# Moving a state transpose, splitting a weight cast and reordering two groups of matmuls in an attention-and-MLP kernel

## The chip, the cores and the metric

The kernel runs on one core of a Trainium2 chip. The metric is the device time in microseconds. Five engines work side by side, each through its own queue in order: TensorE (PE in the profile, with its weight loads as PEld), VectorE (DVE), ScalarE (ACT), GpSimd (POOL) and SyncE (SP, which here only issues DMAs). An instruction that waits holds up all that stands behind it on its engine.

## The reference

`x` has 8 batches of 8 heads with 512 rows of 64, `state` 8 x 8 x 32 x 64. Each attends to the other, and the joined result goes through an MLP:

```python
scores = scale * np.matmul(x, state.transpose(0, 1, 3, 2))
a = softmax(scores)                      # over the 32 states
xread = np.matmul(a, state)
scores2 = scale * np.matmul(state, x.transpose(0, 1, 3, 2))
a2 = softmax(scores2)                    # over the 512 rows of x
sread = np.matmul(a2, x)
y = np.concatenate([xread, sread], axis=2)   # to (8 * 544) tokens x 512
h = y @ w_in                             # 512 x 2048
out = (h * sigmoid(h)) @ w_out           # 2048 x 512
```

(`softmax` stands for the lines that subtract the maximum, take the exponential and divide by the sum.)

## The kernel before, in words

The 512 token columns are cut into 4 pairs of heads (`kt`), the 2048 hidden columns into 16 tiles (`ft`), the 512 x-rows of a batch into 4 output tiles (`tt`). The kernel does not form xread: it folds state into w_in. For each batch it forms `W1 = state @ w_in` (`w1_m` L274, evicted by `w1_e` L299, four quarters `j` of 512 columns), and then `g1` (L309) multiplies the attention weights `aT` with `W1` and ACT applies silu, 128 hidden columns at a time; `g2` (L335) multiplies with `w_out` and sums over `ft` in PSUM. The sread rows are collected in `xsT` and go through the MLP at the end as a ninth batch.

The whole order is written by hand inside `tc.manual_schedule()` (L368): the order of the Python calls is the order of each engine's queue. Waits between engines come from the tiles that instructions share. PSUM has eight banks, `o0 o1 w0 w1 h0 h1 a0 a1`, and calls name the bank they use.

What bears on the change:

- **Loads.** SP issues x of batch 0 in four parts, state 1 into `st_f[1]` (L373), the first quarter of `w_in` in four rows into `w_f` (L375), then a quarter of `w_out` (L430). POOL's queue issues the other weights and x of batches 1 and 2 (L94, L100, L105), between its own casts. From batch 3 on SP issues x (`load_x`, L92), one 1 MB DMA per batch, at L567 and L626, behind the DMA transposes of x (`x_Td`) and among the output stores (`o_e` L354).
- **First softmax (L418 to L463).** Casts of x, PE transposes (`x_T` L139, evicted by `x_Te`), scores (`sc` L171), exponentials (`ex` L183, ACT), row sums and normalisation (DVE and POOL).
- **First W1 (L470 to L478).** `w1f_m` multiplies rows 0 and 1 of `w_f` in fp32. Rows 2 and 3 are cast to bf16 in `w_in_sb` by ACT (L473) and DVE (L474), and `w1_m(0, 0, ..., (2, 3))` reads them. `a_T` (L222) transposes the weights of batch 0 with one eviction on DVE and one on ACT.
- **Start of the MLP (L487 to L500).** `g1(0, 0)`, `g1(0, 1)`, `sread_m` (L239), two more `g1`. On DVE stand the casts of rows 0 and 1 of `w_f` (L491), `sread_n` (L254, which writes `sr`), and the cast of state 1 into `st_nat` (L493). On PE stand `st_T(1)` (L120: a transpose of `st_nat` at L122, two copies into `sbd` by DVE), `G2(0, 0)`, which is `g2` for all four `tt`, and `sread_t` (L264), which transposes `sr`. POOL meanwhile casts four tiles of `w_out_sb` (L468).
- **Batch 1 (L513 to L547).** `cast_x`, `xTs` (L404: two `x_T` and one DVE eviction into `xT`), `scs` (L409), an EXP table load on ACT, `exs` (L400), a SILU table load, `norm_s` and `norm_m` (L193, L198), with `g1` and `G2` of batch 0 between them. `W1x(0, 3, HB, DD)` (L538) forms the last quarter of W1 of batch 0, evicted by two DVE casts.
- **Phases 1 to 8 (L646).** `g2` of one batch with the next batch's steps filled in at the step numbers of `plan` (L613). `soft(b)` casts x of batch b + 1 on POOL (`cast_xu`).

Of the kernel before, what the change touches and what calls it, by code (L numbers as in the profile page):

```python
# [19 lines left out]
def kernel(  # L20
# [8 lines left out]
    nc = tc.nc  # L29
# [13 lines left out]
    st_f = [pers.tile([128, 128], FP32, name=f"st_f{i}") for i in range(2)]  # L43
    w_f = pers.tile([128, KT, 512], FP32, name="w_f")
    wo_f = pers.tile([128, 4, DM], FP32, name="wo_f")
    sbd_f = pers.tile([128, KT, NS], FP32, name="sbd_f")
    st_nat = pers.tile([128, B, 128], BF16, name="st_nat")
# [15 lines left out]
    w_in_sb = pers.tile([128, KT, DF], BF16, name="w_in_sb")  # L63
# [13 lines left out]
    def bf(name):  # L77
        return bank[name][:].bitcast(BF16)

    def cp(eng, dst, src):  # L80
        if eng == "dve":
            nc.vector.tensor_copy(dst, src)  # L82
        elif eng == "pool":
            nc.gpsimd.tensor_copy(dst, src)  # L84
        else:
            nc.scalar.activation(dst, src, func=COPY, bias=0.0)  # L86


    def x_src(b, kt, n):
        return x[b, ds(2 * kt, 2 * n)].rearrange("h (p c) d -> p h (c d)", c=4)  # L90

    def load_x(b, eng, kt=0, n=4):  # L92
        dst = x_f[b % 2][:, ds(kt, n)].rearrange("p k h e -> p (k h) e")
        eng.dma_start(dst, x_src(b, kt, n))  # L94
# [25 lines left out]
    def st_T(b, bk, e0, e1):  # L120
        v = bf(bk)[:, 0:128]
        nc.tensor.transpose(v, st_nat[:, b, :], ident[:])  # L122
        for half, e in ((0, e0), (1, e1)):
            cp(
                e,
                sbd[ds(64 * half, 64), b, :, half, :],
                v[ds(64 * half, 64)].rearrange("p (ns kt) -> p kt ns", kt=KT),
            )
# [10 lines left out]
    def x_T(b, kt, bk):  # L139
        v = bf(bk).rearrange("p (k c t) -> p k c t", k=2, c=4)  # L140
        for c in range(4):
            nc.tensor.transpose(
                v[:, kt % 2, c, :], x_n[b % 2][:, kt, c, ds(2, 128)], ident[:]
            )

    def x_Te(b, kt, n, bk, eng):
        v = bf(bk).rearrange("p (k c t) -> p k c t", k=2, c=4)
        cp(eng, xT[b % 2][:, ds(kt, n)], v[:, ds(kt % 2, n)])
# [22 lines left out]
    def sc(b, kt, bk):  # L171
        v = bank[bk][:].rearrange("p (k h c s) -> p k h c s", k=2, h=2, c=4)
        for c in range(4):
            nc.tensor.matmul(  # L174
                v[:, kt % 2, :, c, :],
                xT[b % 2][:, kt, c, :],
                sbd[:, b, kt, :, :],
                start=True,
                stop=True,
                skip_group_check=True,  # L180
            )

    def ex(b, kt, n, bk):  # L183
        v = bank[bk][:].rearrange("p (k q s) -> p k q s", k=2, q=8)
        nc.scalar.activation(  # L185
            en[b % 2][:, :, :, ds(kt, n), :].rearrange("p h c k s -> p k (h c) s"),
            v[:, ds(kt % 2, n)],
            func=EXP,
            bias=0.0,
            scale=SCALE,  # L190
        )
# [6 lines left out]
    def norm_m(b, eng, kt=0, n=4, h0=0, hn=2):  # L198
        e = nc.vector if eng == "dve" else nc.gpsimd
        e.tensor_tensor(  # L200
            an[b % 2][:, ds(h0, hn), :, ds(kt, n), :].rearrange("p h c k s -> p (h c) k s"),
            en[b % 2][:, ds(h0, hn), :, ds(kt, n), :].rearrange("p h c k s -> p (h c) k s"),
            rs[b % 2][:, ds(h0, hn), :, ds(kt, n)]
            .rearrange("p h c k -> p (h c) k")
            .unsqueeze(3)
            .to_broadcast([128, 4 * hn, n, NS]),
            op=MULT,
        )
# [13 lines left out]
    def a_T(b, bks):  # L222
        n = 2 // len(bks)
        for i, (bk, e) in enumerate(bks):
            v = bf(bk).rearrange("p (h c t) -> p h c t", h=2, c=4)
            for half in range(n):
                for c in range(4):
                    nc.tensor.transpose(
                        v[:, half, c, :], an[b % 2][:, i * n + half, c, :, :], ident[:]
                    )  # L230
            cp(e, aT[b % 2][:, ds(i * n, n)], v[:, ds(0, n)])
# [55 lines left out]
    def w1f_m(bks, kt):  # L287
        for half in range(2):
            nc.tensor.matmul(
                bank[bks[half]][ds(32 * kt, 32), :],  # L290
                sbd_f[ds(64 * half, 64), kt, :],
                w_f[ds(64 * half, 64), kt, :],
                start=True,
                stop=True,
                skip_group_check=True,
                tile_position=(64 * half, 32 * kt),
            )
# [11 lines left out]
    def g1(b, ft):  # L309
        bk = bank[f"h{hctr[0] % 2}"]  # L310
        hctr[0] += 1
        if b < B:
            for half in range(2):
                nc.tensor.matmul(  # L314
                    bk[:],
                    W1[b % 2][:, half, ds(128 * ft, 128)],
                    aT[b % 2][:, half, :, :],
                    start=(half == 0),
                    stop=(half == 1),
                    skip_group_check=True,  # L320
                )
            nc.scalar.activation(g[b % 2][:, ft, :], bk[:], func=SILU, bias=0.0)  # L322
        else:
            for kt in range(KT):
                nc.tensor.matmul(  # L325
                    bk[:, 0:256],
                    w_in_sb[:, kt, ds(128 * ft, 128)],
                    xsT[:, kt, :, :, :],
                    start=(kt == 0),
                    stop=(kt == KT - 1),  # L330
                    skip_group_check=True,
                )
            nc.scalar.activation(g_s[:, ft, :], bk[:, 0:256], func=SILU, bias=0.0)  # L333

    def g2(b, tt, ft, bk, cols=(0, 512)):  # L335
        src = g[b % 2] if b < B else g_s
        c0, c1 = cols
        nc.tensor.matmul(  # L338
            bank[bk][:, c0:c1],
            src[:, ft, ds(128 * tt, 128)],  # L340
            w_out_sb[:, ft, c0:c1],
            start=(ft == 0),
            stop=(ft == 15),
            skip_group_check=True,
        )
# [15 lines left out]
    def warm(n, bk, w=128):  # L361
        for i in range(n):
            nc.tensor.matmul(
                bank[bk][:, 0:w], zeros[:, 0:128], zeros[:, 0:w], start=True, stop=True,
                skip_group_check=True,
            )

    with tc.manual_schedule():  # L368
# [23 lines left out]
        def G2(b, ft):  # L392
            for tt in range(4):
                g2(b, tt, ft, OB[tt])
# [9 lines left out]
        def xTs(b, q, eng):  # L404
            for kt in (2 * q, 2 * q + 1):
                x_T(b, kt, AB[q])
            x_Te(b, 2 * q, 2, AB[q], eng)
# [40 lines left out]
        x_Te(0, 2, 1, XB[2], "dve")  # L448
        sc(0, 1, SB[1])
        ex(0, 1, 1, SB[1])  # L450
        x_T(0, 3, XB[3])
        x_Te(0, 3, 1, XB[3], "dve")
        red(1)
# [14 lines left out]
            cp("pool", w_out_sb[:, i, :], wo_f[:, i, :])  # L468
        nc.scalar.preload_act_table(SILU)
        warm(1, "o0", 512)  # L470
        w1f_m(("w0", "w1"), 0)
        w1f_m(("w0", "w1"), 1)
        cp("act", w_in_sb[:, 2, 0:512], w_f[:, 2, :])  # L473
        cp("dve", w_in_sb[:, 3, 0:512], w_f[:, 3, :])  # L474
        a_T(0, (("a0", "dve"), ("a1", "act")))
        w1_m(0, 0, ("w0", "w1"), (2, 3))
        w1_e(0, 0, ("w0", "w1"), ("act", "dve"), 0, 256)
# [12 lines left out]
        for kt in range(2):  # L490
            cp("dve", w_in_sb[:, kt, 0:512], w_f[:, kt, :])  # L491
        sread_n(0, "a1")
        cp("dve", st_nat[:, 1, :], st_f[1][:])  # L493
        g1(0, 2)
        g1(0, 3)
        st_T(1, "a0", "dve", "dve")
        G2(0, 0)
        sread_t(0, "a1", "dve")
        G2(0, 1)
# [20 lines left out]
        G2(0, 7)  # L520
        g1(0, 9)
        xTs(1, 0, "dve")
        g1(0, 10)
        xTs(1, 1, "dve")
        g1(0, 11)
        scs(1, 0)
        scs(1, 1)
# [6 lines left out]
            load_st(b)  # L534
        G2(0, 8)
        G2(0, 9)
        G2(0, 10)
        W1x(0, 3, HB, DD)  # L538
        norm_s(1, 2, 2)
        norm_m(1, "dve", 2, 2)  # L540
        G2(0, 11)
        g1(0, 12)
        g1(0, 13)
# [20 lines left out]
        g1(1, 4)  # L564
        for tt in range(4):
            o_e(0, tt, OB[tt], "dve")
        load_x(3, nc.sync)  # L567


        TB = ("w0", "o0", "w1", "o1")  # L570
# [2 lines left out]
        def add(step, *fs):  # L573
            fill.setdefault(step if isinstance(step, tuple) else int(step), []).extend(fs)

        def L(f, *a):
            return lambda: f(*a)
# [44 lines left out]
        for b, (sx, ss, sq, se, tl, sr_, sg, dg) in plan.items():  # L622
            if sx is not None:
                add(sx, L(x_Td, b))
                add(ss, L(x_nu, b), L(st_T, b, "a0", "dve", "dve"))
            if 3 < b + 1 < B:  # L626
                add(sx or 74, L(load_x, b + 1, nc.sync))
            add(sq, L(scs, b, 0))
            add(sq + 2, L(scs, b, 1))
            add(se, L(soft, b))  # L630
            add((tl,), L(tiled, b, tl))
            add(sr_, L(sread_x, b, tl))
            for i in range(16):
                add(sg + dg * i, L(g1, b, i))
# [56 lines left out]
```

## Time and profile before

| | us |
|---|---|
| median of the 9 runs | 218.8 (217.7 to 219.77) |
| the profiled execution | 219.77 |
| its span in the profile | 218.0 |
| PE busy | 210.5 |
| ACT busy | 135.2 |
| DVE busy | 84.9 |
| POOL busy | 45.0 |
| granted PE clock (share of full speed) | 1.00 to 204 us, 0.99 behind it |

The profile is of one execution; its times count from the start of the span. A busy PE is one with a matmul in its pipeline. Matmuls overlap: a 128x512 bf16 one lasts 0.38 us, and one follows the other every 0.216 us. "Idle before" an instruction is put down to the engine that released it last. The chain of work that ended last is followed back from the last instruction, at each step to what released it, or to the instruction before it on its engine.

### The profile page before, as it was taken

How to read it: one execution, taken by the hardware profiler on the slowest of the kernel's cores; microseconds unless marked ns; L12 is line 12 of the kernel's file. 1: busy time of each engine (PE TensorE's matmuls, PEld its weight loads, DVE VectorE, ACT ScalarE, POOL GpSimd, SP SyncE). 2: the span in 40 equal slices, each digit the busy share in tenths (PEclk: the TensorE clock that was granted, in tenths of full speed). 3: DMA queues.
4: the chain of work that ended last, by engine and by line, in shares of the span. 5: the costliest groups of instructions: out<-in, count | busy, mean ns of one | idle time of the engine just before them, and what ended most of it. 6: DMA issues, size and time to landing. Idle time of an engine off the chain costs nothing.

```text
span 218.0 us, 4086 instructions
## 1 busy us (share of the span) xinstructions
PE 210.5 (97%) x1655; PEld 104.3 (48%) x1655; DVE 84.9 (39%) x175; ACT 135.2 (62%) x226; POOL 45.0 (21%) x86
## 2 busy tenths in 40 slices
PE   7979999999999999999999999999999999999993
PEld 7523353454444444444444444544454444566553
DVE  3784537841930363248313840276017501111110
ACT  3762576679767947894689458855885586233211
POOL 3696208400700070016001600070001000000000
PEclk9999999999999999999999999999999999999999
DMA  6999994694394139315931593146012311111112
GB/s 192 273 272 261 243 276 71 88 272 147 102 236 145 51 99 247 140 48 119 207 111 48 149 226 112 51 110 147 35 48 42 107 48 48 51 48 48 48 51 96
DMA packets 37363, 27.86 MB, mean 128 GB/s; under 512 B 21984, under 2 KB 31584, under 8 KB 37344
## 3 DMA queue, kind: packets, MB, share of 16 engines
q1 hardware_dynamic: 31280, 21.63, 35.8%
q0 software_dynamic: 5360, 5.44, 12.7%
q10 hardware_dynamic: 704, 0.52, 0.7%
q8 instruction: 13, 0.21, 0.4%
q14 instruction: 6, 0.05, 0.1%
HBM read 17.30 MB, written 8.91 MB: 120 GB/s over the span
## 4 chain that ended last, share of the span: by engine, by line
PE 90%; DVE 3%; DMA 3%; SPq 2%; issue 1%; ACT 0%; DVEq 0%; ACTq 0%
PE ps_o L338 28%; PE ps_w L338 26%; PE ps_h L314 25%; PE ps_h L325 3%; DMA w_f<-in_moe_w_in_dram 3%; PE ps_a L174 1%; DVE w_in_sb L82 1%; PE ps_a L277 1%; PE ps_w L277 1%; DVE W L82 1%; PE ps_o L277 1%; SPq L94 1%; PE ps_h L277 1%; SPq L375 1%; PE ps_o L244 1%
## 5 line engine op out<-in xcount | busy, mean ns | idle before, releaser
L322 ACT ACTIVATE g<-ps_h 128x512 bf16<-128x512 f32 x128 | 75.9, 597 | 35.4 <-PE ps_h L314 28.8
L314 PE MATMUL ps_h<-aT,W 128*128 128x512 bf16 x256 | 75.5, 379 | 0.2 <-DVE W L82 0.2
L338 PEld LDWEIGHTS <-g 128*128 128x128 bf16 x512 | 49.1, 98 | 54.8 <-issue 2.2
L338 PE MATMUL ps_w<-w_out_sb,g 128*128 128x512 bf16 x256 | 73.3, 379 | 0.0
L338 PE MATMUL ps_o<-w_out_sb,g 128*128 128x512 bf16 x256 | 65.9, 379 | 0.2
L314 PEld LDWEIGHTS <-W 128*128 128x128 bf16 x256 | 24.1, 98 | 27.8 <-DVE W L82 1.6
L200 POOL TENSOR_TENSOR an<-en,rs 128x512 bf16<-128x512 bf16 x8 | 8.4, 1056 | 111.7 <-ACT en L185 72.4
L82 DVE COPY o_sb<-ps_w 128x512 f32<-128x512 f32 (+1 forms) x13 | 8.5, 659 | 53.1 <-PE ps_w L338 53.0
L82 DVE COPY o_sb<-ps_o 128x512 f32<-128x512 f32 x14 | 9.5, 687 | 29.6 <-PE ps_o L338 29.5
L84 POOL CAST x_u<-x_f 128x256 bf16<-128x256 f32 x44 | 18.1, 456 | 0.0
L195 DVE TENSOR_REDUCE rs<-en 128x16 f32<-128x512 bf16 x14 | 9.3, 661 | 15.4 <-ACT en L185 15.3
L333 ACT ACTIVATE g_s<-ps_h 128x256 bf16<-128x256 f32 x16 | 6.1, 384 | 14.0 <-PE ps_h L325 14.0
L325 PE MATMUL ps_h<-xsT,w_in_sb 128*128 128x256 bf16 x64 | 9.6, 273 | 0.0
L82 DVE CAST W<-ps_a 128x512 bf16<-128x512 f32 x12 | 8.1, 684 | 2.8 <-PE ps_a L277 2.8
L86 ACT ACTIVATE o_sb<-ps_o 128x512 f32<-128x512 f32 (+1 forms) x4 | 2.2, 544 | 10.7 <-PE ps_o L338 7.9
L185 ACT ACTIVATE en<-ps_a 128x512 bf16<-128x512 f32 (+1 forms) x16 | 8.3, 568 | 0.5 <-PE ps_a L174 0.5
L325 PEld LDWEIGHTS <-w_in_sb 128*128 128x128 bf16 x64 | 6.3, 98 | 4.1
L185 ACT ACT_TABLE_LOAD x6 | 7.7, 1283 | 0.1
L604 ACT ACT_TABLE_LOAD x6 | 7.7, 1283 | 0.1
L86 ACT ACTIVATE o_sb<-ps_w 128x512 f32<-128x512 f32 (+1 forms) x5 | 2.7, 533 | 8.2 <-issue 6.6
L174 PEld LDWEIGHTS <-xT 128*128 128x128 bf16 x128 | 5.9, 98 | 3.7 <-DVE xT L82 0.7
L82 DVE CAST W<-ps_h 128x512 bf16<-128x512 f32 x9 | 6.1, 683 | 2.2 <-PE ps_h L277 2.2
(88 smaller groups left out, 168.6 us busy)
## 6 DMA issues: line engine op xcount, KB each, us to landing
out_dram<-o_sb SPq DMA_DIRECT2D x32, 256.0 KB, 2.7
x_f<-in_x_dram SPq DMA_DIRECT2D x5, 1024.0 KB, 6.7
w_in_sb<-in_moe_w_in_dram POOLq DMA_DIRECT2D x3, 512.0 KB, 10.2
w_out_sb<-in_moe_w_out_dram POOLq DMA_DIRECT2D x3, 512.0 KB, 10.7
x_f<-in_x_dram SPq DMA_DIRECT2D x4, 256.0 KB, 4.0
w_f<-in_moe_w_in_dram SPq DMA_DIRECT2D x4, 256.0 KB, 5.5
wo_f<-in_moe_w_out_dram SPq DMA_DIRECT2D x4, 256.0 KB, 6.6
x_f<-in_x_dram POOLq DMA_DIRECT2D x2, 512.0 KB, 10.0
```

Source lines behind the costliest of these rows:

```text
L82: nc.vector.tensor_copy(dst, src)
L84: nc.gpsimd.tensor_copy(dst, src)
L174: nc.tensor.matmul(v[:, kt % 2, :, c, :], xT[b % 2][:, kt, c, :], sbd[:, b, kt, :, :], start=True, stop=True, skip_group_check=True,)
L185: nc.scalar.activation(en[b % 2][:, :, :, ds(kt, n), :].rearrange("p h c k s -> p k (h c) s"), v[:, ds(kt % 2, n)], func=EXP, bias=0.0, sc ...
L195: nc.vector.tensor_reduce(v, en[b % 2][:, :, :, ds(kt, n), :], axis=AX, op=ADD)
L200: e.tensor_tensor(an[b % 2][:, ds(h0, hn), :, ds(kt, n), :].rearrange("p h c k s -> p (h c) k s"), en[b % 2][:, ds(h0, hn), :, ds(kt, n), ...
L277: nc.tensor.matmul(bank[bks[half]][ds(32 * kt, 32), :], sbd[ds(64 * half, 64), b, kt, half, :], w_in_sb[ds(64 * half, 64), kt, ds(512 * j, ...
L314: nc.tensor.matmul(bk[:], W1[b % 2][:, half, ds(128 * ft, 128)], aT[b % 2][:, half, :, :], start=(half == 0), stop=(half == 1), skip_group ...
L322: nc.scalar.activation(g[b % 2][:, ft, :], bk[:], func=SILU, bias=0.0)
L325: nc.tensor.matmul(bk[:, 0:256], w_in_sb[:, kt, ds(128 * ft, 128)], xsT[:, kt, :, :, :], start=(kt == 0), stop=(kt == KT - 1), skip_group_ ...
L338: nc.tensor.matmul(bank[bk][:, c0:c1], src[:, ft, ds(128 * tt, 128)], w_out_sb[:, ft, c0:c1], start=(ft == 0), stop=(ft == 15), skip_group ...
L604: nc.scalar.preload_act_table(SILU)
```

## The change

It has five parts. (1) The cast of state 1 goes from DVE to ACT and up into the first softmax, behind the second exponential; `st_T(1)` goes up in front of `w1f_m`, and uses bank `o1` and not `a0`. (2) Row 3 of the first w_in quarter is cast by ACT (columns 0 to 255) and DVE (256 to 511), where DVE cast all of it; ACT's part stands ahead of its `aT` eviction. (3) The x transposes of batch 1 follow each other, and `g1(0, 10)` comes behind them. (4) `G2(0, 10)` goes behind `W1x(0, 3)` and the second normalisation. (5) x of batches 3 to 7 is loaded in two DMAs of two `kt` each, where it was one.

```diff
@@ first softmax
         ex(0, 1, 1, SB[1])
+        cp("act", st_nat[:, 1, :], st_f[1][:])
         x_T(0, 3, XB[3])
@@ first W1
         warm(1, "o0", 512)
+        st_T(1, "o1", "dve", "dve")
         w1f_m(("w0", "w1"), 0)
         w1f_m(("w0", "w1"), 1)
         cp("act", w_in_sb[:, 2, 0:512], w_f[:, 2, :])
-        cp("dve", w_in_sb[:, 3, 0:512], w_f[:, 3, :])
+        cp("act", w_in_sb[:, 3, 0:256], w_f[:, 3, 0:256])
+        cp("dve", w_in_sb[:, 3, 256:512], w_f[:, 3, 256:512])
         a_T(0, (("a0", "dve"), ("a1", "act")))
@@ start of the MLP
         sread_n(0, "a1")
-        cp("dve", st_nat[:, 1, :], st_f[1][:])
         g1(0, 2)
         g1(0, 3)
-        st_T(1, "a0", "dve", "dve")
         G2(0, 0)
@@ batch 1
         xTs(1, 0, "dve")
+        xTs(1, 1, "dve")
         g1(0, 10)
-        xTs(1, 1, "dve")
         g1(0, 11)
@@
         G2(0, 9)
-        G2(0, 10)
         W1x(0, 3, HB, DD)
         norm_s(1, 2, 2)
         norm_m(1, "dve", 2, 2)
+        G2(0, 10)
         G2(0, 11)
@@ x loads
-        load_x(3, nc.sync)
+        for kt in (0, 2):
+            load_x(3, nc.sync, kt, 2)
@@
-                add(sx or 74, L(load_x, b + 1, nc.sync))
+                add(sx or 74, *(L(load_x, b + 1, nc.sync, kt, 2) for kt in (0, 2)))
```

## The prediction

> **What bounds the kernel now.** I read first the busy table of the page, then the busy time by stretches, then the chain of work that ended last between 11 and 40 us, and last the timelines of VectorE (DVE), GpSimd (POOL) and ScalarE (ACT) there. The busy table and the stretches (columns: stretch, length, busy us of PE, PEld, DVE, ACT, POOL, clock, DMA share, GB/s):
>
> ```profile
> PE 210.5 (97%) x1655; PEld 104.3 (48%) x1655; DVE 84.9 (39%) x175; ACT 135.2 (62%) x226; POOL 45.0 (21%) x86
> ```
>
> ```profile
> 15.15:16.65 1.50, 0.19 (x1) 0.00 (x1) 1.41 (x4) 0.87 (x2) 1.50 (x4) 1.00 1.25 205
> 16.65:29.43 12.78, 12.78 (x97) 5.58 (x98) 5.79 (x13) 5.47 (x10) 4.48 (x8) 1.00 1.20 245
> 29.43:35.01 5.58, 5.19 (x43) 2.21 (x42) 2.97 (x6) 4.42 (x6) 1.47 (x2) 1.00 0.81 241
> 35.01:60.00 24.99, 24.99 (x235) 11.42 (x236) 15.36 (x32) 18.91 (x31) 9.84 (x19) 1.00 0.62 137
> 60.00:204.00 144.00, 143.81 (x1060) 70.00 (x1058) 48.79 (x96) 94.67 (x157) 18.19 (x37) 1.00 0.38 103
> ```
>
> From 35 us on TensorE (PE) has no hole: there the time is its own work, which the change leaves as it is. Holes that an order can fill lie at 15.15 to 16.65 (1.5 us) and at 29.4 to 35.0 (0.4 us). Whatever moves PE at 35 us moves the end by as much, if nothing with an absolute time (a landing) comes between. The chain through both holes (columns: start, length, what):
>
> ```profile
> 12.56 0.76 DVE W L82 x2
> 13.32 1.14 DVE w_in_sb L82
> 14.46 0.21 issue
> 14.67 1.39 DVE w_in_sb L82
> 16.06 0.08 DVE srec L256
> ...
> 16.17 0.29 DVE sr L257
> 16.46 0.14 DVE st_nat L82
> 16.61 0.04 issue
> 16.65 0.23 PE ps_a L122
> ...
> 29.52 0.70 DVE xT L82
> ...
> 33.68 1.29 DVE W L82 x2
> 34.97 0.05 issue
> 35.01 0.82 PE ps_h L314 x3
> ```
>
> PE stands at the state transpose (L122), which waits for the cast of st_nat, which stands in DVE's queue behind two w_in_sb casts of 1.4 us. Those are slow only there: the same form took 0.43 us at 11.64; here POOL casts w_out_sb beside them.
>
> ```profile
> 13.23 2.83 DVE L82 CAST w_in_sb<-w_f 128x512 bf16<-128x512 f32 x2
> ```
>
> **Part 1, the state cast and transpose.** PE issues the fourth matmul of g1(0,3) at 14.29 + 4 x 0.216 = 15.15. Without the transpose, G2(0,0) comes next. Its inputs are there: g of ft 0 by 14.2 (ACT, 13.61 + 0.60), w_out_sb 0 by 13.9 (POOL, 13.27 + 0.6). It takes 0.86 (16.72 to 17.58 now), so 15.15 to 16.01. What is late next is sread_t, which needs sr: 16.17 + 0.29 = 16.46, and PE starts 0.05 behind its releaser (16.61 to 16.65), so 16.51; 0.06 later G2(0,1) starts, at 16.57 where it was 17.64. **Gain 1.07**; 0.5 of the hole stays. From zero (DVE later by as much) to 1.56 (sr no longer late: G2(0,1) at 16.08).
>
> Where the moved pieces go: the ACT cast (0.31, as for state 0) falls into ACT's wait of 0.45 before 8.54; state 1 landed at 2.80 + 4.4 = 7.2. The transpose (about 0.1 of PE) falls before w1f_m; the second pair there waits for its landing until 9.65 and a_T for POOL's product until 10.78. The two copies into sbd (2 x 0.29) meet DVE's idle 0.98 before 11.64 and leave 0.40. All three cost nothing; without cover they would add at most the 0.58 of the copies. Bank o1 is read again by 11.3, 4 us before G2 writes it.
>
> **Part 2, w_in_sb row 3 by two engines.** Its landing at 11.61 starts the chain; DVE now ends at 12.07. DVE's half takes 0.29 (128x256 cast). ACT's half lies between the 0.31 of 128 columns and the 0.63 of 512, by the straight line 0.42: end 12.06. ACT becomes the one that counts, and nothing is gained. Behind it ACT's aT eviction slips from 11.47 to 11.97; W's first ACT piece could then start at 12.47 (evictions follow each other at 0.50: 20.18, 20.67) and starts at 12.53 anyway. **0**; from -0.14 (ACT as fast as DVE's 0.29) to +0.2 (ACT at 0.63).
>
> **Part 3, x transposes in a row, W1x(0,3) ahead of G2(0,10).** In times of before: x_T(1,1) at 28.37 instead of 28.80, so DVE's xT copies start at 28.57 and, 0.60 behind, 29.17, and end at 29.86; the two g1 (0.43 each) lie between, and the last scores start at 29.92 instead of 30.27. But the next wait is not PE's: ACT's silu of ft 10 starts at 29.45 instead of 29.00, that of ft 11 at 29.94 instead of 29.88, so table load, exponentials (31.79) and DVE's norm_s come 0.05 later. W's casts now stand behind norm_s alone: its reciprocal ends at 33.39 + 0.05, they start at 33.46 instead of 33.68, though W1x's matmuls are 0.86 earlier. PE is released 0.22 earlier than 35.01. **Gain 0.22**; from 0 to 0.40, all of PE's idle there. Behind those casts on DVE stand norm_s, norm_m and W(1,2) in the old order, so a_T(1) keeps its margin.
>
> **Part 4, x loads in halves.** Five more issues on SP. One 1 MB issue kept SP 0.39 to 1.29 us, a 256 KB one about 0.5, so a second half adds from nothing to 1.3. Behind it stand output stores (four o_sb buffers, one used each 5.7 us, a quarter of the 22.9 from phase to phase) and, 16 us on (61.27, 77.95), the aT transpose. The loads land 6.1 to 7.2 us after issue; the casts that read them come 3.9 us later for x 3 (46.13 + 6.5 against 56.55) and at least 8.8 for the others. **0**; it shows only if a half lands 3.9 us later than the whole. The Trainium skill speaks against this part ("DMA: Bandwidth & Descriptors", Rules for kernel authors: 1 MiB or more per DMA for bandwidth). By it the halves would be slower; with the 3.9 us between landing and use the sum stays the same, and no run here shows 512 KB from SP.
>
> **Sum:** 1.07 + 0 + 0.22 + 0 = 1.29 us. The profiled execution took 219.77 (span 218.0 and 1.77 around it); changed, 218.5 (span 216.7). It was the slowest of the nine shown, 0.97 over their median; off the median 218.8 the same gain gives **217.5 us**.
>
> **Rivals.** (a) *The two casts change turns.* DVE is ready for the first at 13.31, POOL starts its four casts at 13.27. If part 2 makes DVE ready 0.05 sooner, the first takes 0.43 and not 1.4, sr is about 1 us earlier, and part 1 gives its cap of 1.56: 218.8 - 1.78 = 217.0. For it: 0.04 us decide. Against: part 2 gains nothing by my sum. Here the skill ("SBUF — State Buffer", Who interferes with whom) says that whoever starts first locks a shared port pair for one whole instruction; a DVE cast would then wait for one POOL cast, 1.0 in all, and the rows of 1.39 and 1.51 show two. By that rule sr would be at about 15.6 after a won first turn.
>
> (b) *Little is left.* A third POOL cast (0.61) slips ahead of a DVE cast, and part 2 costs 0.15: part 1 gives 0.3, in all 0.5: 218.3. Against: DVE's start moves by under 0.2 by my sum, and two casts precede it already.
>
> (c) *Slower: a POOL queue landing becomes the bound.* With PE 1.07 earlier, w_in_sb's second quarter (issued 7.51, landed 16.9) is read at 18.6, w_out_sb's (19.4) at 21.2, w_in_sb's third (22.0) at 23.9, x 1's second half, cast by 25.6, at 27.5: 1.7 to 1.9 us to spare. A landing later by 1.7 starts to eat the gain; one later by 1.7 + 1.3 + 0.7 = 3.7 makes it slower by more than 0.3%, 219.6 or more. For it: landings in this queue took 8.4 to 14.3 us, and DMA is at 1.2 of its share there. Against: nothing ahead of these issues on POOL moves.
>
> (d) *The change doesn't do what it says:* the early transpose delays w1f_m or DVE, and the wait goes over to g1(0,0). The uncovered 0.58 less the 0.40 of cover: 0.2, and with no gain of part 3 217.9.
>
> **Chances.** Forecast 0.55 (216.9 to 218.1), (a) 0.15, (b) 0.12, (d) 0.06, (c) 0.12. The range takes in (a), (b) and (d) with run to run scatter of the median: 216.5 to 218.7. A measurement of this kernel tells 0.3%, 0.66 us, from no change: faster means under 218.14, slower over 219.46. Forecast, (a) and part of (d) are faster: 0.74; (b) and the edge of the forecast within: 0.14; (c) slower: 0.12.
>
> **What would show it.** Right: PE's wait at L122 gone, a wait of about 0.5 at the sread transpose (L266) near 16.5, released by sr; the 0.3 at the second scores gone; DVE's W casts for j 3 directly behind norm_s's reciprocal; PE without holes from there on. Wrong: w_in_sb casts of other lengths; the first g1 later than 13.1; PE waiting for a DMA between 18 and 30 us; x_u casts waiting for x_f after 50 us.

## The result and the profile after

| | before | changed |
|---|---|---|
| median, us | 218.72 (63 runs, 217.7 to 219.77) | 217.5 (21 runs, 216.76 to 218.13) |
| ratio to before | 1 | 0.9943 (95%: 0.9932 to 0.9954) |
| profiled execution, us | 219.77 | 217.75 |
| its span, us | 218.0 | 216.0 |

The kernel became 1.25 us faster (1.0 to 1.5), 1.22 by the medians. The forecast was 1.29. The two profiled executions lie 2.0 apart: the profile of before was of an unusually slow execution, and that will matter below.

The busy time of the changed kernel in the two stretches that had holes (columns as before: stretch, length, busy us of PE, PEld, DVE, ACT, POOL, clock, DMA share, GB/s):

```profile
15.15:16.65 1.50, 1.50 (x9) 0.73 (x8) 1.03 (x4) 1.08 (x2) 1.50 (x3) 1.00 1.25 205
29.43:35.01 5.58, 5.38 (x38) 1.93 (x36) 3.75 (x8) 4.71 (x7) 2.73 (x4) 1.00 0.87 244
```

The first hole is gone altogether, where half a microsecond was forecast to stay; of the second, 0.2 is left. The chain of work that ended last (start, length, what):

```profile
11.69 0.59 DVE w_in_sb L82
12.28 0.04 issue
12.32 0.39 PE ps_w L277 x2
...
14.58 0.98 PE ps_h L314 x4
15.55 0.43 PE ps_w L338 x2
15.98 0.43 PE ps_o L338 x2
16.42 0.06 PE ps_a L266
16.47 0.43 PE ps_w L338 x2
...
29.23 1.28 ACT L529
30.51 0.01 issue
30.52 0.61 ACT en L185
31.13 0.02 issue
31.15 0.70 DVE rs L195
31.85 0.02 issue
31.87 0.25 DVE rs L196
32.13 1.15 DVE W L82 x2
33.27 0.05 issue
33.32 0.82 PE ps_h L314 x3
```

From 13.25 to 28 us the chain is PE alone: the sread transpose (L266) follows G2(0,0) without a wait, so sr was not late. Then the chain leaves PE as forecast: table load, exponentials, norm_s, and the two W casts straight behind its reciprocal.

**Where the time went, by stretches.** The medians of single parts scatter too much to be added up (each interval is 0.3 to 0.5 us to either side), but the starts of the same instructions can be compared across profiles. I cut every profiled execution at the same marks, all from ACT, DVE and DMA records: A, landing of row 3 of `w_f` to the first silu (L322); B, to ACT's first W eviction behind it (L86, from ps_h); C, to the first exponential of batch 1 (L185); D, to the silu of ft 13; E, to DVE's last output copy; F, to the end of the span.

| kernel | A | B | C | D | E | F |
|---|---|---|---|---|---|---|
| before | 1.99 | 6.57 | 11.61 | 4.14 | 178.50 | 3.56 |
| changed | 2.16 | 5.03 | 11.67 | 3.72 | 178.49 | 3.26 |
| part 1 alone | 2.12 | 5.03 | 11.61 | 4.15 | 178.58 | 3.57 |
| part 2 alone | 1.98 | 5.37 | 11.61 | 4.14 | 178.58 | 3.59 |
| part 3 alone | 1.99 | 5.44 | 11.67 | 3.72 | 178.49 | 3.58 |
| part 4 alone | 1.99 | 6.50 | 11.61 | 4.15 | 178.49 | 3.26 |

Part 1 is B, part 3 is C and D, and part 4 is F, which the forecast had not looked at. E, 82% of the span, hardly moves.

### The profile page after: what moved, and what is told of

The parts are those of the page before. It is cut to its first block, busy times and chain, and to the rows that moved or that the text cites. A ratio compares the mean times of both kernels' runs of the same rounds, so it can differ in the third digit from the quotient of the medians.

```text
span 216.0 us, 4098 instructions
## 1 busy us (share of the span) xinstructions
PE 209.5 (97%) x1655; PEld 103.7 (48%) x1655; DVE 84.8 (39%) x174; ACT 135.7 (63%) x228; POOL 44.9 (21%) x86
## 3 DMA queue, kind: packets, MB, share of 16 engines
q0 software_dynamic: 5360, 5.44, 12.8%
## 4 chain that ended last, share of the span: by engine, by line
PE 90%; DMA 3%; SPq 2%; ACT 1%; DVE 1%; issue 1%; ACTq 0%
PE ps_o L338 27%; PE ps_w L338 26%; PE ps_h L314 26%; PE ps_h L325 3%; DMA w_f<-in_moe_w_in_dram 3%; PE ps_a L174 1%; PE ps_a L277 1%; PE ps_w L277 1%; SPq L94 1%; PE ps_o L277 1%; SPq L375 1%; PE ps_o L244 1%; PE ps_h L277 1%; ACT L529 1%; DVE W L82 1%
## 5 line engine op out<-in xcount | busy, mean ns | idle before, releaser
L322 ACT ACTIVATE g<-ps_h 128x512 bf16<-128x512 f32 x128 | 75.8, 597 | 35.2 <-PE ps_h L314 28.5
L86 ACT ACTIVATE o_sb<-ps_o 128x512 f32<-128x512 f32 (+1 forms) x4 | 2.2, 544 | 10.7 <-PE ps_o L338 7.9
L185 ACT ACTIVATE en<-ps_a 128x512 bf16<-128x512 f32 (+1 forms) x16 | 8.3, 568 | 0.3 <-PE ps_a L174 0.2
L86 ACT ACTIVATE o_sb<-ps_w 128x512 f32<-128x512 f32 (+1 forms) x5 | 2.7, 534 | 8.2 <-issue 6.6
L277 PEld LDWEIGHTS <-sbd 64*32 64x32 bf16 x252 | 3.6, 90 | 6.5 <-issue 3.6
```

The lines of the kernel that those rows point to most:

```text
L185: nc.scalar.activation(en[b % 2][:, :, :, ds(kt, n), :].rearrange("p h c k s -> p k (h c) s"), v[:, ds(kt % 2, n)], func=EXP, bias=0.0, sc ...
L277: nc.tensor.matmul(bank[bks[half]][ds(32 * kt, 32), :], sbd[ds(64 * half, 64), b, kt, half, :], w_in_sb[ds(64 * half, 64), kt, ds(512 * j, ...
```

## The experiments

### One part at a time

```diff
 e1_state (before, with)
+cp("act", st_nat[:, 1, :], st_f[1][:])     # behind ex(0, 1, ...)
+st_T(1, "o1", "dve", "dve")                # ahead of w1f_m
-cp("dve", st_nat[:, 1, :], st_f[1][:])
-st_T(1, "a0", "dve", "dve")
```

> Only part 1: the cast of state 1 by ACT in the first softmax and its transpose ahead of w1f_m; the rest as before. Theory S (the sum on record): 1.07 us less than before, 217.65, and PE waiting near 16.5 for sr. Rival T (the profile after, where the hole was gone and G2(0,1) started 1.33 earlier): part 1 alone is worth 1.3, 217.4, and sr is not late. Rival C (the wait goes over to the first g1): under 0.5.

Measured 217.98, ratio 0.9977 (0.9961 to 0.9993), about 0.5 less. B is 5.03, as in the changed kernel. PE waits neither for the state cast nor for sr. Theory T describes the trace; the gain of 1.3 that it added to that does not follow, since before's own B is not always 6.57 (next group).

```diff
 e2_half_cast (before, with)
-cp("dve", w_in_sb[:, 3, 0:512], w_f[:, 3, :])
+cp("act", w_in_sb[:, 3, 0:256], w_f[:, 3, 0:256])
+cp("dve", w_in_sb[:, 3, 256:512], w_f[:, 3, 256:512])
```

> Only part 2: row 3 of the first w_in quarter cast by ACT and DVE in halves. Theory S: no change, 218.7 (between -0.14 and +0.2). Rival T: in the profile after, DVE's half took 0.58 us and ended at 12.28, where the whole took 0.43 and ended at 12.07; if that is what the half does each time, the first g1 and all behind it are 0.2 later, 218.9.

218.82, ratio 1.0016 (0.9998 to 1.0034); A is 1.98 against 1.99. ACT's half ends last and ends as late as the whole did. No gain.

```diff
 e3_order (before, with)
 xTs(1, 0, "dve")
+xTs(1, 1, "dve")
 g1(0, 10)
-xTs(1, 1, "dve")
...
-G2(0, 10)
 W1x(0, 3, HB, DD)
 norm_s(1, 2, 2)
 norm_m(1, "dve", 2, 2)
+G2(0, 10)
```

> Only part 3: the two x transposes in a row and G2(0,10) behind W1x(0,3). Theory S: 0.22 us less, 218.5. Rival T (the profile after, where the two W casts took 1.15 behind the reciprocal and PE was released 1.69 earlier, of which 1.33 were there before): 0.36 less, 218.35. Rival C: no gain, the exponentials set the time alone.

218.54, ratio 1.000 (0.9978 to 1.0022): the time alone cannot tell. In the trace C is 0.06 longer and D 0.42 shorter, a net 0.36, as rival T had it.

```diff
 e4_halves (before, with)
-load_x(3, nc.sync)
+for kt in (0, 2):
+    load_x(3, nc.sync, kt, 2)
 (and the same at the loads of x 4 to 7)
```

> Only part 4: x of batches 3 to 7 loaded in two DMAs each. Theory S: no change, 218.7, x_u casts wait for no x. Rival C: the second issue holds up SP, stores or transposes come late and PE waits in the phases behind 60 us: over 0.3 more. Rival D: the end of the span, where the last store lands, changes.

218.18, ratio 0.9973 (0.9952 to 0.9994). E is as before: no cast into `x_u` waits for its load of x, and PE waits for nothing new. But F is 3.26 and not 3.56. Rival D was the right one, put down without a mechanism. The group on the end of the program finds it.

### What made the hole, and how large it is

Part 4 alone leaves the hole as it was, and shows the queue well. The timelines of DVE and POOL in that execution (start, length, engine, line, operation):

```profile
12.76 2.18 DVE L82 CAST w_in_sb<-w_f 128x512 bf16<-128x512 f32 x2
14.86 0.15 DVE L256 RECIPROCAL srec<-ps_a 128x2 f32<-128x2 f32 x1
15.05 0.29 DVE L257 TENSOR_TENSOR sr<-ps_a,srec 128x128 bf16<-128x128 f32 x1
15.26 0.79 DVE L82 CAST st_nat<-st_f 128x128 bf16<-128x128 f32 x1
12.62 0.77 POOL L94 DMA_DIRECT2D x_f<-in_x_dram  x1
13.37 2.59 POOL L84 CAST w_out_sb<-wo_f 128x512 bf16<-128x512 f32 x4
```

Here the two casts take 2.18 and the small state cast 0.79, where the profile of before had 2.83 and 0.22. POOL casts w_out_sb from 13.37 to 15.96. So the hole depends on which DVE instruction meets which POOL instruction. Two kernels test that.

```diff
 f1_cast_first (before, with)
+cp("dve", st_nat[:, 1, :], st_f[1][:])
 for kt in range(2):
     cp("dve", w_in_sb[:, kt, 0:512], w_f[:, kt, :])
 sread_n(0, "a1")
-cp("dve", st_nat[:, 1, :], st_f[1][:])
```

> The kernel before, with only the cast of state 1 put ahead of the two w_in_sb casts on DVE; the transpose stays where it was. In the profiles so far the stretch from the first silu to the first W eviction of ACT behind it takes 5.4 to 6.6 us where the state cast stands behind those casts, and 5.03 with part 1. Theory Q (the hole is the place in DVE's queue behind casts that POOL slows; where the transpose stands hardly matters): 5.1, and a median near that of part 1 alone, 218.0. Rival (the transpose and its copies are the cost): over 5.4, 218.5 or more.

217.91, ratio 0.9983 (0.9971 to 0.9996). B is 5.08. Its DVE timeline:

```profile
12.62 0.22 DVE L82 CAST st_nat<-st_f 128x128 bf16<-128x128 f32 x1
12.75 1.63 DVE L82 CAST w_in_sb<-w_f 128x512 bf16<-128x512 f32 x2
```

In this execution the two casts took only 1.63. Beside casts as short (1.62 and 1.67, in two kernels with the state cast behind them) B was 5.39 and 5.44, so the line moved took away 0.31 to 0.36 of the 0.36 to 0.41 that part 1 (5.03) would have taken. The hole was a place in DVE's queue; where the transpose stands is worth 0.05. Theory Q holds; with long casts no profile shows it, but the median (217.91) is near that of part 1 alone (217.98).

```diff
 f2_pool_later (before, with)
 load_x(1, nc.gpsimd, 0, 2)
+load_x(1, nc.gpsimd, 2, 2)      # ahead of the four w_out_sb casts
...
-load_x(1, nc.gpsimd, 2, 2)
```

> The kernel before, with POOL's second x load of batch 1 issued ahead of its four w_out_sb casts, so that these start some 0.75 us later than DVE's two w_in_sb casts. Theory L (DVE's casts are long only as POOL's casts come between, and who starts first goes first): the two take about 0.9 to 1.6 us each time and not 2.2 to 2.8, the stretch from the first silu to the W eviction 5.4 or less, the median 0.3 to 0.9 less than before. Rival (the casts are slow for another reason, the landings beside them): 2.2 to 2.8 as in before, no gain.

218.61, ratio 0.9999 (0.9979 to 1.002); the casts 2.19, B 5.95. Theory L fails as it was put. POOL's first cast began at 13.45, only 0.2 later than in the profile of before, since all of POOL's work was earlier in this execution; the first DVE cast took 0.89, the second 1.38. The first began 0.62 ahead of POOL's casts and still took twice its 0.43. It ended at 13.72, 0.25 behind the end of POOL's DMA issues (11.96 to 13.48). Three more profiles show the same: in those of `e4_halves` (above), `e9_xts` and `e10_w1x` the first cast began 0.6 ahead of POOL's casts, took 0.88 to 0.89 and ended 0.25 behind the end of POOL's DMA issue. In `e5_no_half` and `f1_cast_first` a cast beside the same issue took 0.42 to 0.46, and the issue 0.89 to 0.91 where it takes 0.77. By these times POOL's DMA issues can hold DVE up as its casts do; this is read from where the casts end, and no run takes the issue away.

What all the runs do settle is the scatter. In seven profiles with the state cast behind those casts B was 5.37, 5.39, 5.44, 5.94, 5.95, 6.50 and 6.57, a mean of 5.88 (the two casts took 1.53 to 2.83). In the six with part 1 (those told of further down among them) it was 5.03 to 5.06, with casts of 0.98 to 2.32. Part 1 is thus worth 0.3 to 1.5 us in one execution, 0.85 in the mean, and takes the scatter out of this stretch.

### Part 2 in the changed kernel

```diff
 e5_no_half (changed, with)
-cp("act", w_in_sb[:, 3, 0:256], w_f[:, 3, 0:256])
-cp("dve", w_in_sb[:, 3, 256:512], w_f[:, 3, 256:512])
+cp("dve", w_in_sb[:, 3, 0:512], w_f[:, 3, :])
```

> The changed kernel without part 2: DVE casts all of row 3. From the landing of that row to the first silu: 1.98 to 1.99 us in four profiles, 2.12 with part 1 alone, 2.16 in the changed kernel. Theory S: part 2 is worth nothing, 217.5, 2.0 to 2.15 us. Rival H (the half on ACT costs 0.15): 217.35, 1.99. Rival G (part 2 gains 0.1): 217.6.

217.75, ratio 0.997 (0.995 to 0.999), against 0.9943 (0.9932 to 0.9954) with it: the intervals touch. A is 2.21. In this execution row 3 landed early, at 11.01, and DVE was still at part 1's copies into sbd until 11.21 (first line); it cast the row behind them:

```profile
10.63 0.58 DVE L82 COPY sbd<-ps_o 64x128 bf16<-64x128 bf16 x2
11.25 0.43 DVE L82 CAST w_in_sb<-w_f 128x512 bf16<-128x512 f32 x1
```

So the copies, costed at nothing under a cover of 0.40, delay the cast by 0.2 when the landing comes 0.6 earlier. Not all of that reaches A: in `f1_cast_first`, where row 3 landed at 11.00 and no copies stood in the way, A was 2.09, since the transposes of `a_T` ended only at 11.48. Against that profile the copies cost 0.12. Whether the split helps then is open: A with the split and part 1 was 2.16, 2.16, 2.02 and 1.98, without the split and with part 1 2.12 and 2.21. With the split DVE's half took 0.57 and 0.58 in the two profiles at 2.16, 0.43 at 2.02 and 0.29 at 1.98. The traces show no more than 0.1; the medians would allow some 0.6 for it beside part 1, and deny any gain when it stands alone.

### The end of the program

In part 4 alone and in the changed kernel the last 3.56 us are 3.26. The trace has the events of SP's sequencer at the close of the program. For before and changed (us from the end of the span; the semaphore that SP checks):

```
before:  last store issued -3.25, lands -1.22 on semaphore 104
  -2.52 check 100   -2.05 check 102   -1.21 check 104   -1.15 check 105
  -1.09 check 107   -1.02 check 108   -0.97 check 109   -0.90 check 110
changed: last store issued -2.94, lands -0.91 on semaphore 110
  -2.21 check 100   -2.15 check 102   -2.08 check 104   -2.02 check 105
  -1.96 check 107   -1.90 check 108   -1.75 check 109   -0.89 check 110
```

SP checks eight DMA semaphores in a fixed order. DMAs take them in turn. In before the last store had the third, and five checks of 0.06 us came behind its landing. Five DMAs more move it to the eighth, and nothing is left to check. That would have to go the other way with one DMA more:

```diff
 f4_one_more (changed, with)
-for kt in (0, 2):
-    load_x(3, nc.sync, kt, 2)
+for kt, n in ((0, 2), (2, 1), (3, 1)):
+    load_x(3, nc.sync, kt, n)
```

> The changed kernel with one DMA more: x of batch 3 in three parts. Theory W: SP closes the program by checking the DMAs' semaphores one after the other, 0.06 us each, and each further DMA moves the last store one on in that ring of eight; with five more it is the last to be checked, and the end comes 0.31 sooner (3.26 us from DVE's last copy to the end, against 3.56). With six more the last store is the first in the list, and the other seven checks come behind its landing: 3.26 + 7 x 0.06 = 3.7 us, 217.9. Rival (halves end the span sooner because their data land sooner): 3.26 and 217.5 as in the changed kernel.

F is 3.71, against 3.7 expected by theory W and 3.26 by its rival; the last store lands on semaphore 100, at -1.34, and seven checks follow. 217.71, ratio 0.9971 (0.9956 to 0.9986): the median lies between the two expected, the ratio above the 0.9943 (0.9932 to 0.9954) of the changed kernel. Part 4's gain is the number of DMAs; that its data come in halves has nothing to do with it. The landings of the halves (median 5.1 us, where the whole took 6.7) were needed by nobody.

### The two halves of part 3, and one step further

```diff
 e9_xts  (before, with only)          e10_w1x (before, with only)
 xTs(1, 0, "dve")                     -G2(0, 10)
+xTs(1, 1, "dve")                      W1x(0, 3, HB, DD)
 g1(0, 10)                             norm_s(1, 2, 2)
-xTs(1, 1, "dve")                      norm_m(1, "dve", 2, 2)
                                      +G2(0, 10)
```

> The kernel before with only the two x transposes in a row, G2(0,10) in its old place. Theory S: W's casts would still begin behind norm_s's reciprocal, PE's matmuls for them being there by then, so this alone brings what part 3 brings: from the exponentials to the silu of ft 13 about 3.85 (4.15 before, 3.72 with both). Rival (the place of W1x matters as well): 4.0 or more.

> The kernel before with only W1x(0,3) ahead of G2(0,10). Theory S: DVE's W casts begin behind the reciprocal and not behind PE's matmuls, 0.27 earlier, and PE is released 0.3 to 0.4 earlier: 3.72 to 3.85 from the exponentials to the silu of ft 13, whether or not the x transposes are in a row; then either half of part 3 does for both. Rival (PE's stall at the scores goes on): 4.15.

Ratios 0.9985 (0.9966 to 1.0005) and 0.9989 (0.9972 to 1.0005), times that tell little. The traces: C + D is 15.75 before, 15.41 with the x transposes alone, 15.36 with W1x alone, 15.39 with both. Either half brings it all, since either makes the matmuls for W early enough, and then the reciprocal of norm_s sets the casts. The x transposes in a row only add the 0.06 in C.

```diff
 f5_w1x_early (changed, with)
+G2(0, 8)
+W1x(0, 3, HB, DD)
 norm_s(1, 0, 2)
 norm_m(1, "pool", 0, 2)
...
-G2(0, 8)
-W1x(0, 3, HB, DD)
```

> The changed kernel with G2(0,8) and W1x(0,3) still further ahead, in front of norm_s(1,0,2): DVE makes the two W casts while it waits for the exponentials (2.6 us of idle there in the changed kernel), and norm_s comes behind them. Theory N (PE's last wait there, 0.37 between the two halves of g1(0,12), is the W casts behind the reciprocal): the stretch from the exponentials to the silu of ft 13 falls from 3.72 to 3.35, the median to 217.15. Rival (the late norm_s makes the weights' transposes late): the gain is taken back, 3.7 or a longer stretch behind it.

217.81, ratio 0.9966 (0.995 to 0.9983): not better than the changed kernel. The wait for the W casts is gone, and another took its place. The chain that ended last:

```profile
17.52 12.81 DMA w_in_sb<-in_moe_w_in_dram
30.33 0.04 issue
30.38 0.41 PE ps_h L277 x8
```

PE now waits 0.34 for the last quarter of w_in, issued by POOL at 17.52 and landed at 30.33. D is 3.75, no shorter than 3.72. This is rival (c) of the prediction, one step beyond the change. And the changed kernel is close to it: the quarter landed 0.97 before it was read in its first profile (29.69, 30.66), and before had 3.5 to spare (29.68, 33.19). In `e5_no_half` 0.17 was left. In `f4_one_more`, whose order is that of the changed kernel up to 40 us, PE did wait, since POOL's last `w_out_sb` cast had waited 2.26 for a landing and the quarter was issued only at 19.65:

```profile
30.74 0.41 PE L277 MATMUL ps_h<-w_in_sb,sbd 64*32 64x512 bf16 x8 [0.33 <-DMA w_in_sb<-in_moe_w_in_dram]
```

D was 3.74 there. The wait stood where PE would have waited for the W casts a little later, so that it cost next to nothing. The chain that ended last runs through this landing in that profile, so a later one would have cost.

```diff
 f6_changed_again: the changed kernel, no edit
```

> The changed kernel once more, beside the others on this chip: 217.5, ratio 0.994. The stretch from the first silu to ACT's W eviction 5.03 us again (4.95 to 5.1), where kernels with the state cast behind the w_in_sb casts had 5.37, 5.44, 5.95, 6.50 and 6.57; the end 3.26 behind DVE's last copy.

217.42, ratio 0.994 (0.9917 to 0.9963); B 5.03, F 3.28, and the last quarter landed 0.59 ahead of its reader. None of the other kernels was faster.

## Why the prediction was right, step by step

The time and the sign were right (217.5). The sum was right in size, but its terms were not: part 1, with its A, fell short by 0.34, parts 3 and 4 gave 0.14 and 0.31 more. That these misses cancel to about 0.1 is luck.

| step | forecast | in the traces |
|---|---|---|
| part 1, state | -1.07 | -0.85 in the mean of seven executions against six (B), and +0.12 in A |
| part 2, half cast | 0 | 0 alone; open beside part 1 |
| part 3, order | -0.22 | -0.36 |
| part 4, halves | 0 | -0.31 |
| sum | -1.29 | -1.40; by the runs -1.25 (-1.5 to -1.0) |

- **Part 1.** The mechanism held: the state cast's place in DVE's queue. The size was worked out from one execution, in which the two casts took 2.83, the longest of fourteen profiles. "0.5 of the hole stays" fell: sr is late only if the casts take more than some 2.35 (in the execution with 2.32 it came 0.03 ahead of need), and that came up in no execution with part 1. So the step gained 1.54 against that execution, and 0.85 against the usual one, while the sum took the forecast off the median. That the forecast of 1.07 came near the mean is chance: an overlong hole and a remainder that did not exist worked against each other. Rival (a), put as a 0.15 chance in the changed kernel, is in truth a scatter of each execution, of before as well. (Its 15.6 for sr comes out with both casts at about 1.0; after a won first turn the same terms give about 15.1.)
- **Its cover.** "All three cost nothing" held for the landing at 11.6 of that one profile. Over six profiles with part 1, A is 2.11 in the mean against 1.99 in seven of the eight without (2.09 in the eighth); in one of them the copies are a visible cause. In three the cast of row 3 itself took 0.55 to 0.58 beside POOL's DMA issues; that part 1 brings this about is not shown. So one of the prediction's own signs of being wrong came up in the changed kernel, the first g1 later than 13.1 (13.18), and so did another, casts of other lengths (1.47 and 0.83).
- **Part 2.** "ACT becomes the one that counts" held alone (A 1.98). In the changed kernel's first profile it did not: DVE's half took 0.58, not the 0.29 of the sum, and the chain goes through it (11.69, 0.59).
- **Part 3.** The chain was forecast to the step: table load 0.05 later (C: 0.06), W casts directly behind the reciprocal. The mis-sized term is the two casts. With their input waiting they took 1.15, and PE was released 1.20 behind the reciprocal's end; the sum had 1.35 (34.79 less 33.44), from casts that had started behind a wait.
- **Part 4.** "0; it shows only if a half lands 3.9 us later" looked at the loads' readers, and was right there; in the two profiles both halves had landed 5.7 to 6.9 behind the first issue, the whole 6.1 to 7.2, so the halves were not slower either. The step that failed is that a count of DMAs changes nothing else. The trace of before showed the closing checks, one every 0.06 us, five of them behind the last landing.
- **Rival (c).** Its list of landings left out the last quarter of w_in, whose reader part 3 moves by another 0.86: it had the least to spare.

## What to carry to other kernels

A hole that one engine's contention makes has the size of that execution; look at several executions, or price it by what the order allows (here 5.03 us of PE's own work), before the gain is written down. The cure can be one line in one queue: the cast moved ahead of the two contended ones brought the stretch to 5.08, where part 1 has 5.03, with its reader where it was. An edit in a steady loop that adds or removes DMAs shifts which semaphore the last store lands on, so compare the tail as well as the loop; and list again every landing whose reader an edit moves, since the next bound is the one with the least to spare.

## What the runs showed of the hardware

- A 128x512 fp32-to-bf16 cast on DVE took 0.43 us alone, and 0.41 to 1.51 beside POOL's casts and DMA issues. POOL's casts of the same form took 0.60 to 0.64, and up to 0.85 where a DVE cast ended inside them. The Trainium skill ("SBUF — State Buffer", Who interferes with whom) says that a DVE instruction in a two-port mode, which a cast can enter, and a POOL instruction meet at a shared port pair: whichever issues first has it for its whole length and blocks the other. A DVE cast that waits for one such POOL cast would by that take 1.07 at most, an estimate. The casts of 0.8 to 0.9 agree with it (some behind a POOL cast, those of four profiles behind a DMA issue). The 1.29 to 1.51 seen in eight of the fourteen profiles do not: in seven of them two POOL casts went by first, in the eighth (`f1_cast_first`) a DMA issue and a cast, and each ended 0.28 to 0.29 behind the end of the second.
- The closing checks of DMA semaphores by SP cost 0.06 us each, and up to seven of the eight stood behind the last landing.
- In the profiles of changed and before, two DMAs of 512 KB from SP kept its queue 1.0 to 1.6 us, one of 1 MB 0.4 to 1.3; each half landed 4.2 to 5.9 us after its own issue, the whole after 6.1 to 7.2.
